# Two sums of x made one chunk later, and one `gl` made on GpSimd, in a fused attention and FFN kernel

## The chip, the cores and the metric

The kernel runs on one core of one Trainium2 chip. The metric is the device time of one execution in microseconds (us). Engines are named as the profile does: PE is TensorE (PEld its weight loads), DVE is VectorE, ACT is ScalarE, POOL is GpSimd, SP is SyncE, whose queue issues most DMAs.

## The reference

Linear attention over 8 batches, 8 heads, 576 positions and 64 columns, and a feed-forward layer over its 4608 rows of 512:

```python
q_s = exp(q - max(q, -1)); q_s = q_s / (sum(q_s, -1) + 1e-9)
k_s = exp(k - max(k, 2));  k_s = k_s / (sum(k_s, 2) + 1e-9)
x = q_s @ (k_s.T @ v)            # per batch and head; then 4608 x 512
h = maximum(x @ w_in, 0)         # 512 -> 2048
out = (h * h) @ w_out            # 2048 -> 512
```

All of it is float32.

## The kernel before, in words

**Split products.** A float32 value goes through TensorE as two parts, `hi` (rounded to the format fp32r, by a ScalarE copy) and `lo` (the rest, by a VectorE subtraction). A product of two values is three matmuls: hi x hi, hi x lo and lo x hi. So each operand of a matmul needs one ScalarE instruction and one subtraction before TensorE may read it.

**Tiles and chunks.** The rows are cut into nine tiles of 512: tile t below 8 holds the first 512 positions of batch t, and the ninth gathers the last 64 positions of all batches (`x_tail`). Tiles 0 to 6 go through the loop `for t in range(WT)` with sixteen chunks f of 128 hidden columns each. A chunk is `first` (the product with `w_in` into the PSUM tile `h`, twelve matmuls; then `r` = relu on ScalarE and `h` = relu(h) times r on VectorE), and two chunks later `second` (four times three matmuls into the four PSUM tiles `acc`), with `split_g` making `gh` on ScalarE and `gl` on VectorE as weights of `second`. Into these chunks the attention of the next batch is woven: `turns[t, f]` says which steps (b, s) are done in chunk f. In tile 6 the last of them, step 15 of batch 7, falls in chunk 11. There `step_between` multiplies x for the third pair of heads and splits q of the fourth (`blocks_split`: `qh` on ScalarE, `ql` on VectorE), and `step_after` multiplies x for the fourth pair. `x_product` makes six matmuls, copies one half of the result on ScalarE and the other on VectorE, and then copies 64 columns into `xt` on ScalarE.

**The joint block.** The last two tiles, 7 and 8, are not multiplied one by one. With both halves of the 512 columns of x, and the weights in quarters, seven products do the work of eight (a Strassen scheme). It needs sums of x: t1 = b12 - b11, t2 = b22 - t1, t3 = b11 - t2, t4 = b21 - t2, where b11 and b21 are halves of tile 7 and b12 and b22 halves of tile 8, and each is split into hi and lo. `ahead(f, x)` makes them in the last tile's chunks 4 to 15, at the end of each chunk's instructions; `take` is two VectorE subtractions of 128 x 512, and `split_x_of` two ScalarE casts and two VectorE subtractions. The temporary tiles of t1 are `sum_k` and `sum_q`; the profile calls the pieces of x after their split `w`, since they lie in memory of used weights.

The joint block itself is `for n in range(PAIRS)`, eight pairs of chunks. In a pair, seven `product` calls of six matmuls each (L1193) go into two PSUM tiles, and between them `unit` calls do the `second` products of the pair before, or, in the first pair, those of tile 6 that are left. `use_g` makes relu squared in place on VectorE (tile `c`), then `gh` on ScalarE and `gl` on the engine that it is given, for the two chunks that are used at once; `keep_g` writes the other two to memory for tile 8. The `gh` and `gl` of pair 0 are read first by the units of pair 1.

**What sets the order.** Tile 0 is ordered by a planner that simulates the engines (`Planner`). From tile 1 on each engine runs its instructions in the order in which the program states them, so a waiting instruction holds back all that stands behind it on its engine. Most instructions carry line 100 in the profile, the helper that issues them (the joint block's and the loop's), and are told apart by tile names.

Of the kernel before, what the change touches and what calls it, by code (L numbers as in the profile page):

```python
# [336 lines left out]
def attention_ffn(  # L337
# [75 lines left out]
    V, S, G = Engine(plan, nc.vector, 0.14, 0.00108), Engine(plan, nc.scalar, 0.18, 0.00087), Engine(plan, nc.gpsimd, 0.1, 0.0021)  # L413
# [693 lines left out]
    def weights(n):  # L1107

        if n >= PAIRS:
            return None  # L1110
        if n % 2 == 0:
            quads = [slabs[i].rearrange("p t (i c) -> p (t i) c", c=HM) for i in (0, 1, 14, 15)]
            w = {}
            for q, names in enumerate((("s1", "a11"), ("s2", "a12"), ("s3", "a22"), ("s4",))):
                for i, name in enumerate(names):
                    w[name] = quads[q][:, 2 * i:2 * i + 2, :]
        else:
            big = att.tile([P, 4, M], F32R, tag="x_next", name=f"ring_{n}")
            big = big.rearrange("p t (i c) -> p (t i) c", c=HM)
            w = {name: big[:, 2 * i:2 * i + 2, :] for i, name in enumerate(("s1", "a11", "s2", "a12"))}  # L1120
            for name, tag in (("s3", "qn"), ("a22", "qh"), ("s4", "ql")):
                w[name] = att.tile(
                    [P, 2, HM], F32R, tag=tag, name=f"ring_{name}_{n}", bufs=None if tag == "qn" else 1
                )
        return w
# [4 lines left out]
    def load_weights(n, w, *names):  # L1130

        for name in names if w else ():
            if n >= OWN and name in SUMS:
                continue
            at = SOURCE[name]
            Y.dma_start(out=w[name].bitcast(F32), in_=w_sums[n][:, at:at + 2, :])
# [52 lines left out]
    def product(out, w, x, begin, end=True):  # L1189
        (wh, wl), (xh, xl) = (w[:, 0, :], w[:, 1, :]), x  # L1190
        for k in range(2):
            for i, (a, m) in enumerate(((wh, xh), (wh, xl), (wl, xh))):
                nc.tensor.matmul(  # L1193
                    out=out.real(), lhsT=a[:, k * P:(k + 1) * P].real(), rhs=m[k].real(),
                    start=(begin and k == 0 and i == 0), stop=(k == 1 and i == 2),
                    skip_group_check=True,
                )
# [240 lines left out]
    def take(name, eng, out, in0, in1):  # L1438

        for i in range(2):  # L1440
            eng.tensor_tensor(out=out[i], in0=in0[i], in1=in1[i], op=ALU.subtract)
        made[name] = out

    def split_x_of(name):

        x_of[name] = pieces(name, 0)
        for i in range(2):
            split_part(made[name], name, i)

    def ahead(f, x):  # L1450

        k = range(2)
        if f == 4:
            made["b11"] = [x[:, i, :] for i in k]
            made["b21"] = [x[:, 2 + i, :] for i in k]
            made["b12"], made["b22"] = (
                [slabs[X_RAW + j].bitcast(F32)[:, i, :] for i in k] for j in range(2)
            )
            for i in k:
                to = slabs[X_RAW + i].bitcast(F32)[:, :, 0:(B - 1) * TL]  # L1460
                Y.dma_start(out=to, in_=x_tail[:, 2 * i:2 * i + 2, 0:(B - 1) * TL])
            w_of[0] = weights(0)
            load_weights(0, w_of[0], "a11", "s1", "a12", "s2")
        elif f == 6:
            split_x_of("b11")
        elif f == 10:
            temps = [att.tile([P, M], F32, tag=tag, name=f"sum_{tag}") for tag in ("k", "q")]
            take("t1", V, temps, made["b12"], made["b11"])
        elif f == 11:
            split_x_of("t1")  # L1470
        elif f == 12:
            split_x_of("b21")
            take("t2", V, made["t1"], made["b22"], made["t1"])
        elif f == 13:
            split_x_of("t2")
            take("t3", V, made["b11"], made["t2"], made["b11"])
        elif f == 14:
            split_x_of("t3")
            take("t4", V, made["b21"], made["b21"], made["t2"])
        elif f == 15:  # L1480
            load_weights(0, w_of[0], "s3", "a22", "s4")
            split_x_of("b22")
# [16 lines left out]
    for t in range(WT):  # L1499
        x_next, acc = begin_next(t), begin_acc(t)  # L1500
        parts = {}
        for f in range(NF):
# [29 lines left out]
            if t == WT - 1:  # L1532
                ahead(f, x_next)
# [12 lines left out]
    def unit(count):  # L1546

        for t, f, parts_u, acc_u, c, begin, end in units[:count]:
            second(f, parts_u, acc_u, c, begin=begin, end=end)
            if f == end:  # L1550
                store(t, acc_u, c)
        del units[:count]
# [6 lines left out]
    def use_g(f, c, tags, eng):  # L1559

        V.scalar_tensor_tensor(out=c, in0=c, scalar=0.0, in1=c, op0=ALU.max, op1=ALU.mult)
        split_last(f, c, tags, eng, WT)

    def split_last(f, c, tags, eng, t):

        gh, gl = (
            pool_of.tile([P, M], F32R, tag=tag, name=f"{kind}_{t}_{f}", bufs=bufs)
            for kind, (pool_of, tag, bufs) in zip(("gh", "gl"), tags)
        )
        S.copy(out=gh, in_=c)  # L1570
        eng.tensor_tensor(out=gl, in0=c, in1=gh, op=ALU.subtract)
        parts[t, f] = gh, gl

    one_tags = ((ffn, "gh", None), (ffn, "gl", None))
# [9 lines left out]
    for n in range(PAIRS):  # L1584
        one, two = 2 * n, 2 * n + 1
        units_at = (0, 1, 1, 1, 1) if n else (3, 0, 1, 0, 0)
        w = w_of.pop(n)
        w_next = w_of.get(n + 1)
        own_sums(n + 1, w_next, 0)
        A, Bk = (ps_h.tile([P, M], F32, tag="h", name=f"h_{WT}_{f}") for f in (two, one))  # L1590
        u1, u2, u3 = (
            ffn.tile([P, M], F32, tag=tag, name=f"u_{tag}_{n}", bufs=1) for tag in ("xh2", "xl2", "xh3")
        )
        c11, c21 = (ffn.tile([P, M], F32, tag="r", name=f"c_{WT}_{f}") for f in (one, two))
        c22, c12 = (att.tile([P, M], F32, tag="ek", name=f"c_{B}_{f}", bufs=2) for f in (two, one))
        if n == 0:
            split_x_of("t4")
        unit(units_at[0])

        product(A, w["a11"], x_of["b11"], True)  # L1600
        S.copy(out=u1, in_=A)
        unit(units_at[1])
        product(Bk, w["a12"], x_of["b21"], True)
        V.tensor_tensor(out=c11, in0=Bk, in1=u1, op=ALU.add)
        use_g(one, c11, one_tags, V)
        own_sums(n + 1, w_next, 1)
        if n == PAIRS - 1:
            load_g(0)
            load_g(1)
        unit(units_at[2])  # L1610
        product(A, w["s2"], x_of["t2"], False)
        S.copy(out=u2, in_=A)
        own_sums(n + 1, w_next, 2)
        if n == 0:
            w_of[1] = weights(1)
            load_weights(1, w_of[1], "a11", "s1", "a12", "s2", "s3", "a22", "s4")
        elif n + 2 < PAIRS:
            w_of[n + 2] = weights(n + 2)
        unit(units_at[3])
        product(Bk, w["s1"], x_of["t1"], True)  # L1620
        if n == 0:
            w_of[2] = weights(2)
        load_weights(n + 2, w_of.get(n + 2), "a12", "s2", "a11", "s1")
        own_sums(n + 1, w_next, 3)
        unit(units_at[4])
        product(A, w["s3"], x_of["t3"], False)
        S.copy(out=u3, in_=A)
        V.tensor_tensor(out=c22, in0=Bk, in1=u3, op=ALU.add)
        keep_g(two, c22)
        own_sums(n + 1, w_next, 4)  # L1630
        if n == PAIRS - 1:
            load_g(2)
        unit(2)
        product(A, w["a22"], x_of["t4"], False)
        load_weights(n + 2, w_of.get(n + 2), "s3", "a22")
        S.copy(out=c21, in_=A)
        own_sums(n + 1, w_next, 5)
        unit(1)
        product(Bk, w["s4"], x_of["b22"], False)
        load_weights(n + 2, w_of.get(n + 2), "s4")  # L1640
        V.tensor_tensor(out=c12, in0=Bk, in1=u2, op=ALU.add)
        tags = ((att, "v", 2), (att, "k" if n % 2 else "q", None))
        use_g(two, c21, tags, V)
        keep_g(one, c12)
        own_sums(n + 1, w_next, 6)
        if n == PAIRS - 1:
            load_g(3)
        unit(1)
        if acc is None:
            acc = begin_acc(WT)  # L1650
        units += [(WT, f, parts[WT, f], acc, c, 0, NF - 1) for f in (one, two) for c in range(C)]
# [54 lines left out]
```

## Time and profile before

| | |
|---|---|
| three runs | 876.64, 876.74, 879.33 us |
| median | 876.74 us |
| the profiled execution | 876.96 us, span 875.2 us |
| TensorE busy | 853.2 us |
| VectorE busy | 582.5 us |
| ScalarE busy | 379.4 us |
| GpSimd busy | 124.4 us |
| mean granted TensorE clock | 0.999 |

The span runs from the first to the last recorded instruction; the execution's own time is 1.76 us more. A row of a timeline gives start, duration, engine, line, operation, output and inputs, and in brackets how long the engine was idle before and who ended that. A row of a view of waits gives who waited for whom, microseconds in total, how often, and the longest. In a row of the chain that ended last, start and duration count only the part of an instruction that lies on the chain.

### The profile page before, as it was taken

What the parts mean: (1) busy time and instruction counts of PE and PEld (TensorE: products, weight loads), DVE (VectorE), ACT (ScalarE), POOL (GpSimd) and SP (SyncE); (2) the same over time, 40 slices, a digit from 0 to 9 for tenths busy, and PEclk for the clock granted to TensorE, in tenths of its full rate; (3) what the DMA queues carried; (4) which work ended last, traced back from release to release, by engine and by line L of the source; (5) the groups of instructions that cost most, each with busy time, mean ns of one, the idle gap of its engine ahead of it and who ended that gap; (6) DMA issues with size and microseconds to landing.
All of it is one profiled execution on the core that took longest, in us unless ns stands there. A gap on an engine that the chain in (4) does not pass through costs nothing.

```text
span 875.2 us, 12474 instructions
## 1 busy us (share of the span) xinstructions
PE 853.2 (97%) x4408; PEld 703.6 (80%) x4408; DVE 582.5 (67%) x1174; ACT 379.4 (43%) x731; POOL 124.4 (14%) x153
## 2 busy tenths in 40 slices
PE   5889999999999999999999999999999999999997
PEld 4668878888888888888888888888887888888786
DVE  5898896656766667667766566676677656766421
ACT  3888864343534253434534353334343442323321
POOL 4788991000000000000000000000000000000000
PEclk9999999999999999999999999999999999999999
DMA  9991022212331344132340332122341163332432
GB/s 279 382 347 45 25 68 73 76 38 75 93 98 29 87 106 134 39 83 80 95 105 21 87 90 52 27 54 64 87 121 31 38 204 109 105 102 69 156 113 49
DMA packets 157071, 86.08 MB, mean 98 GB/s; under 512 B 112720, under 2 KB 141392, under 8 KB 157008
## 3 DMA queue, kind: packets, MB, share of 16 engines
q1 hardware_dynamic: 155296, 83.97, 33.6%
q10 hardware_dynamic: 1712, 1.31, 0.6%
q8 instruction: 35, 0.57, 0.3%
q14 instruction: 28, 0.23, 0.1%
HBM read 60.16 MB, written 24.51 MB: 97 GB/s over the span
## 4 chain that ended last, share of the span: by engine, by line
PE 89%; DVE 4%; DMA 3%; SPq 3%; ACT 1%; issue 0%; DVEq 0%; ACTq 0%
PE acc L100 43%; PE h L100 32%; PE h L1193 9%; SPq L100 3%; PE x L100 3%; PE kv L100 2%; DMA raw<-in_moe_w_out_dram 1%; DMA q<-in_q_dram 1%; DVE bst L100 1%; DVE km L100 1%; DVE h L100 1%; DMA kt<-in_k_dram 0%; DVE gl L100 0%; DMA bst<-bst 0%; DVE q L100 0%
## 5 line engine op out<-in xcount | busy, mean ns | idle before, releaser
L100 PE MATMUL acc<-w,gh 128*128 128x512 f32 x1152 | 355.8, 390 | 0.0
L100 PE MATMUL h<-xh,w 128*128 128x512 f32 x896 | 295.8, 392 | 2.3 <-DVE gl L100 2.3
L100 PEld LDWEIGHTS acc<-w,gh 128*128 128x128 f32 x1152 | 214.7, 188 | 43.9 <-ACT gh L100 0.4
L100 PE MATMUL acc<-w,gl 128*128 128x512 f32 x576 | 224.2, 389 | 0.0
L100 PEld LDWEIGHTS h<-xh,w 128*128 128x128 f32 x896 | 168.2, 188 | 38.4 <-DVE gl L100 2.4
L100 PE MATMUL h<-xl,w 128*128 128x512 f32 x448 | 174.5, 389 | 0.0
L100 PEld LDWEIGHTS acc<-w,gl 128*128 128x128 f32 x576 | 108.1, 188 | 23.1 <-DVE gl L100 0.4
L100 DVE TENSOR_TENSOR gl<-h,gh 128x512 fp32r<-128x512 f32 x112 | 77.1, 689 | 71.2 <-ACT gh L100 61.7
L100 ACT ACTIVATE gh<-r 128x512 fp32r<-128x512 f32 x112 | 70.7, 631 | 92.7 <-PE acc L100 90.3
L100 DVE SCALAR_TENSOR_TENSOR h<-h,r 128x512 f32<-128x512 f32 x112 | 77.2, 690 | 45.2 <-ACT r L100 44.6
L100 PEld LDWEIGHTS h<-xl,w 128*128 128x128 f32 x448 | 84.1, 188 | 16.3
L100 ACT ACTIVATE r<-h 128x512 f32<-128x512 f32 x112 | 66.4, 593 | 65.2 <-PE h L100 64.9
L100 POOL PARTITION_ALL_REDUCE kmx<-km x24 | 16.9, 703 | 509.2 <-DVE km L100 509.2
L100 ACT ACTIVATE q<-q 128x576 f32<-128x576 f32 (+1 forms) x32 | 21.6, 674 | 70.3 <-DVE q L100 62.3
L100 DVE TENSOR_REDUCE bst<-q 128x18 f32<-128x576 f32 x48 | 35.9, 748 | 13.9 <-ACT q L100 13.5
L100 POOL TENSOR_TENSOR w<-w,raw 128x512 int32<-128x512 int32 x32 | 42.1, 1325 | 6.5 <-DVE w L100 3.7
L100 POOL TENSOR_TENSOR w<-w,w 128x512 fp32r<-128x512 f32 x32 | 41.1, 1299 | 4.7 <-ACT w L100 4.5
L100 DVE TENSOR_TENSOR q<-q,bst 128x576 f32<-128x576 f32 x48 | 36.4, 758 | 1.7
L100 ACT ACTIVATE raw<-raw 128x1024 f32<-128x1024 f32 (+1 forms) x32 | 36.3, 1148 | 0.1
L1193 PE MATMUL h<-w,w 128*128 128x512 f32 x144 | 36.0, 389 | 0.0
L100 DVE TENSOR_TENSOR bst<-bst 128x18 f32<-128x18 f32 (+1 forms) x96 | 17.8, 186 | 23.6 <-DMA bst<-bst 14.8
L100 DVE TENSOR_TENSOR ql<-qT,qh 128x576 fp32r<-128x576 f32 (+1 forms) x32 | 23.6, 739 | 14.1 <-ACT qh L100 12.9
(163 smaller groups left out, 893.6 us busy)
## 6 DMA issues: line engine op xcount, KB each, us to landing
k<-in_k_dram SPq DMA_DIRECT2D x32, 256.0 KB, 2.9
raw<-in_moe_w_in_dram SPq DMA_DIRECT2D x16, 512.0 KB, 8.7
raw<-in_moe_w_out_dram SPq DMA_DIRECT2D x16, 512.0 KB, 9.4
out_dram<-o SPq DMA_DIRECT2D x32, 256.0 KB, 2.4
w_sums<-w SPq DMA_DIRECT2D x30, 256.0 KB, 3.1
v<-in_v_dram SPq DMA_DIRECT2D x56, 128.0 KB, 3.0
q<-in_q_dram SPq DMA_DIRECT2D x96, 72.0 KB, 2.3
w<-w_sums SPq DMA_DIRECT2D x16, 256.0 KB, 3.7
```

The lines of the kernel that those rows point to most:

```text
L100: getattr(self.eng, op)(*map(real, args), **{k: real(a) for k, a in kwargs.items()})
L1193: nc.tensor.matmul(out=out.real(), lhsT=a[:, k * P:(k + 1) * P].real(), rhs=m[k].real(), start=(begin and k == 0 and i == 0), stop=(k == 1 ...
```

## The change

Two edits in the last stretch of the kernel. The `take` of t1 moves from the end of chunk 10 of tile 6 to the end of chunk 11, directly in front of t1's split, which was in chunk 11 already. And in the joint block's pair 0 the subtraction that makes `gl` of the pair's first chunk (`use_g(one, ...)`) is issued on GpSimd; in pairs 1 to 7 it stays on VectorE.

```diff
         elif f == 6:
             split_x_of("b11")
-        elif f == 10:
+        elif f == 11:
             temps = [att.tile([P, M], F32, tag=tag, name=f"sum_{tag}") for tag in ("k", "q")]
             take("t1", V, temps, made["b12"], made["b11"])
-        elif f == 11:
             split_x_of("t1")
         elif f == 12:
             split_x_of("b21")
...
         V.tensor_tensor(out=c11, in0=Bk, in1=u1, op=ALU.add)
-        use_g(one, c11, one_tags, V)
+        use_g(one, c11, one_tags, V if n else G)
         own_sums(n + 1, w_next, 1)
```

## The prediction

> **What bounds the kernel now.** I read the page first, for the share of each engine; then TensorE's waits from the last batch's end on; then the chain that ended last around the place of the change; then the timelines of TensorE, VectorE and ScalarE there. The page:
>
> ```profile
> span 875.2 us, 12474 instructions
> ## 1 busy us (share of the span) xinstructions
> PE 853.2 (97%) x4408; PEld 703.6 (80%) x4408; DVE 582.5 (67%) x1174; ACT 379.4 (43%) x731; POOL 124.4 (14%) x153
> ```
>
> TensorE is busy for 97% of the span, VectorE for 67%, GpSimd for 14%. So VectorE's time counts only where TensorE waits for it. All waits of TensorE's matmuls from 660 us to the end of the span:
>
> ```profile
> PE x L100 <- ACT qh L100: 0.5, 1, 0.5
> PE x L100 <- DVE ql L100: 0.3, 1, 0.3
> ```
>
> There are two, both at the last product of x (tile `x`, of `x_product`) before the joint block. Everything else after 660 us runs back to back on TensorE; what makes these two shorter ends the kernel earlier, and nothing else there does. The chain that ended last says what they hang on (start, duration, what):
>
> ```profile
> 674.22 0.69 DVE sum_k L100
> 674.91 0.60 DVE sum_q L100
> 675.51 0.03 issue
> 675.54 0.70 DVE h L100
> 676.24 0.30 DVE x L100
> 676.57 0.21 ACT xt L100
> 676.80 0.68 ACT qh L100
> 677.51 0.77 DVE ql L100
> ```
>
> `sum_k` and `sum_q` are the "first two sums of x": the two subtractions of `take("t1")`. They stand on VectorE in front of chunk 11's `h` and of the copy of `x`. The copy releases `xt` on ScalarE, behind `xt` stands `qh`, behind `qh` comes `ql` on VectorE, and TensorE needs `qh` and `ql`. So the sums are on the path that sets the end, from 674.22 to 675.51: 1.29 us. TensorE meanwhile (start, duration):
>
> ```profile
> 674.68 0.29 PE L100 MATMUL x<-ql,kvh 128*128 128x288 f32 x1
> ...
> 676.65 0.39 PE L100 MATMUL acc<-w,gl 128*128 128x512 f32 x1
> 677.53 0.40 PE L100 MATMUL x<-qh,kvh 128*128 128x288 f32 x1 [0.49 <-ACT qh L100]
> ...
> 678.32 0.40 PE L100 MATMUL x<-ql,kvh 128*128 128x288 f32 x1 [0.26 <-DVE ql L100]
> ...
> 678.95 0.40 PE L100 MATMUL h<-xh,w 128*128 128x512 f32 x1
> ```
>
> From the start of the last `acc` matmul (676.65) to chunk 12's first `h` matmul (678.95) it takes 2.30 us. The same stretch, undisturbed by sums, stands in the trace at the product of the same batch's other two pairs of heads, some chunks earlier:
>
> ```profile
> 640.30 0.39 PE L100 MATMUL acc<-w,gl 128*128 128x512 f32 x1
> 640.53 0.29 PE L100 MATMUL x<-qh,kvh 128*128 128x288 f32 x1
> 640.66 0.29 PE L100 MATMUL x<-qh,kvl 128*128 128x288 f32 x1
> 640.83 0.40 PE L100 MATMUL x<-ql,kvh 128*128 128x288 f32 x1
> ...
> 641.47 0.39 PE L100 MATMUL h<-xh,w 128*128 128x512 f32 x1
> ```
>
> There the same six matmuls and the step to `h` take 641.47 - 640.30 = 1.17 us. Their `ql` was made here:
>
> ```profile
> 638.65 0.39 DVE L100 COPY x<-x 128x224 f32<-128x224 f32 x1
> 640.01 0.76 DVE L100 TENSOR_TENSOR ql<-qT,qh 128x576 fp32r<-128x576 f32 x1 [0.97 <-ACT qh L100]
> ```
>
> **The change part by part. First part, the sums one chunk later.** What is taken out of chunk 11 is 1.29 us of VectorE in front of `h`. How early can the chain then start? ScalarE's rows around it:
>
> ```profile
> 673.60 0.60 ACT L100 ACTIVATE r<-h 128x512 f32<-128x512 f32 x1
> ...
> 679.69 0.62 ACT L100 CAST w<-sum_k 128x512 fp32r<-128x512 f32 x1
> 680.21 0.62 ACT L100 CAST w<-sum_q 128x512 fp32r<-128x512 f32 x1
> 681.88 0.60 ACT L100 ACTIVATE r<-h 128x512 f32<-128x512 f32 x1 [1.05 <-PE h L100]
> 684.44 0.63 ACT L100 ACTIVATE gh<-r 128x512 fp32r<-128x512 f32 x1 [1.96 <-PE acc L100]
> ```
>
> Chunk 11's `r` ends at 674.20, and VectorE comes free for the first sum at 674.22; so `h` can start there instead, near 674.24, and end near 674.94. The copy of `x` after it needs the `x` matmul of 674.68, which ends at 674.97: the copy starts near 675.02, set by TensorE now and no longer by VectorE. In the undisturbed block, from the start of the copy (638.65) to the end of `ql` (640.77) it is 2.12 us, which holds the rest of the copy, `xt`, `qh` and `ql`. That puts the end of `ql` at 677.14. TensorE used it 0.06 us after its end there, so at 677.20 here. Measured from the last `acc` matmul: there 640.83 - 640.30 = 0.53 us; here 676.65 + 0.53 = 677.18. The two agree within 0.02 us, so I take the undisturbed block as the model for the whole stretch: chunk 12 starts at 676.65 + 1.17 = 677.82 in place of 678.95. The gain is 1.13 us.
>
> Both ends: at best `ql` does not bind at all, and the six matmuls follow at the step of 640.53 to 640.66, 0.13 us, after a first step of 0.23 (640.30 to 640.53); 0.23 + 6 x 0.13 = 1.01 us, a gain of 1.29. At the low end only the idle time that the view of waits names is won, 0.49 + 0.26 = 0.75 us; the rest, 0.38 us, is the slower start of the pipelined matmuls after each halt, which should go with the halts. Below nothing this term can't go unless the sums cost more at their new place, which comes next.
>
> The Trainium skill says the same about idle time of TensorE (Perfetto Trace Analysis, Identifying the Most-Contended Engine): busy time of matmuls is a poor measure, since pipelined instructions look smaller. By busy time alone the sum would be 0.75 us, by starts it is 1.13; the trace's own rows above show the difference.
>
> What the sums cost at the new place: they now stand in chunk 11's `ahead`, behind the last copy of `x` and in front of their own split; all of it is VectorE and ScalarE work, there are no DMAs with them, and no queue of SP or GpSimd is passed. Behind them on VectorE: the two `lo` subtractions, then chunk 12's `h`. Behind the casts on ScalarE: chunk 12's `r`. The copy's row of before is
>
> ```profile
> 679.16 0.39 DVE L100 COPY x<-x 128x224 f32<-128x224 f32 x1 [0.29 <-PE x L100]
> ```
>
> Moved by 1.13 it ends at 678.42. The sums then take 678.45 to 679.74 by the 1.29 above. The casts wait for them one by one: the first may start near 679.2, the second near 679.77, and it ends near 680.4. Chunk 12's `r` waited for TensorE until 681.88; moved, that is 680.75. So ScalarE is free 0.35 us before it is wanted, and the cost is nothing. If that cover were gone, the next one is the wait of 1.96 us in front of `gh` (684.44), where ScalarE waits for TensorE: the sums would have to come 2.3 us later than reckoned before anything that TensorE reads moved.
>
> **Second part, `gl` of chunk 0 of the joint block on GpSimd.** It takes one instruction from VectorE and gives it to GpSimd:
>
> ```profile
> 707.91 0.69 DVE L100 TENSOR_TENSOR gl<-c,gh 128x512 fp32r<-128x512 f32 x1 [0.74 <-ACT gh L100]
> 711.06 0.69 DVE L100 TENSOR_TENSOR c<-h,u_xh 128x512 f32<-128x512 f32 x1 [2.46 <-ACT u_xh L100]
> ```
>
> After this `gl` VectorE has nothing to do until 711.06, where it waits for ScalarE's `u_xh` and so for TensorE. Taking 0.69 us from it there gains nothing. GpSimd's price of the same shape, and the use of this `gl`:
>
> ```profile
> L100 POOL TENSOR_TENSOR w<-w,w 128x512 fp32r<-128x512 f32 x32 | 41.1, 1299 | 4.7 <-ACT w L100 4.5
> 717.27 0.19 PEld L100 LDWEIGHTS acc<-w,gl 128*128 128x128 f32 x1
> ```
>
> On GpSimd it takes 1.30 us, twice as long: 707.91 + 1.30 = 709.21, and TensorE loads it as a weight first at 717.27, in the next pair. That leaves 8.06 us, which moves with TensorE and so stays. Nothing else is queued on GpSimd there, and VectorE is idle while it runs. The cost is nothing; the cover is those 8.06 us.
>
> **The sum.** -1.13 for the sums, 0 for their new place, 0 for `gl`. The profiled execution took 876.96 us with a span of 875.2, so 1.76 lies around the span. Forecast for it: span 874.07, time 875.83. It stands 0.22 above the median of the runs, 876.74; less 1.13 this gives 875.6.
>
> **The rivals.** First: the halt goes only in part. The copy of `x` could start later than 675.02, since the matmuls in front of it hang on the `kv` parts made just before, and each 0.1 us there costs 0.1. For it speaks that `ql` would arrive within 0.02 us of the moment that it is needed, so there is no room; against it, that the undisturbed block has the same order of work and its `ql` matmul comes only 0.04 us later than the step of 0.13. A gain from 0 to 0.75: 876.0 to 876.7.
>
> Second: the gain is given back, because something that does not move with TensorE turns up late in the joint block, a load of weights say. For it: TensorE would be 1.13 us earlier at every load. Against it: TensorE has not one wait after 678.32 in the view of waits, and loads that refill buffers wait for their readers, which come earlier too. 876.7.
>
> Third, slower: GpSimd brings `gl` too late. This happens at the first second-product of the joint block's chunk 0, at 717.27; it decides from 8.06 us of delay on, each microsecond beyond costs one, and with the 1.13 won before, the kernel is slower than now only from 9.19 us on, and by over 0.3% from 11.8 us on. For it: GpSimd has had no such subtraction since the weights were split. Against it: by the row above, the thirty-two like it took 1299 ns on average, so the delay would have to be over six times the instruction.
>
> The Trainium skill has a rule for this (GPSIMD Engine Reference, Instruction dispatch): the first call to freshly loaded code pays about 6 us that no row shows. By that estimate `gl` would still come 2 us early and the sum is the same; no run here shows such a load for a subtraction after a long pause.
>
> **How the numbers follow.** Forecast 0.83, first rival 0.10, second 0.05, third 0.02. What a measurement of this kernel can tell from no change is about 0.3%, 2.6 us; no case but the third reaches it. So: within 0.3% 0.95; slower 0.03, the third rival and a little for scatter, since one of the three runs of before stands at 879.33; faster 0.02, for something that no row shows. Range: at the low end the best gain from the lowest run, 876.64 - 1.29 = 875.35, and 0.15 for scatter, 875.2; at the high end no gain, 876.74, rounded up to 876.8, which takes in the first two rivals.
>
> **What would show it.** Right: the two waits of `x` on `qh` and `ql` gone or under 0.1 us together, some 1.2 us from the last `acc` matmul to chunk 12's `h`, `sum_k` behind the last copy of `x`, all of TensorE's later work 1.1 us earlier, and one `gl` of about 1.3 us on GpSimd that ends over 7 us before its weight load. Wrong: a wait for `ql` of 0.3 us or more (first rival); a new wait of TensorE in the joint block (second); `acc` waiting for GpSimd's `gl` (third); chunk 12's `r` or `h` late behind the casts, which would break the step on the new place.

## The result and the profile after

The changed kernel takes 872.14 us, median of six runs (870.65 to 874.13); before it was 876.75 (876.49 to 879.33). The ratio is 0.9944, interval 0.9925 to 0.9963. Forecast were 875.6 us, range 875.2 to 876.8, no measurable difference: 4.6 us were won where 1.1 were reckoned, and the time lies below the range. The profiled execution took 870.65 us with a span of 868.9, against 876.96 and 875.2. So 6.3 us of span have to be found. They are more than the 4.6 us of the medians because the profiled execution is the fastest of its six, 1.5 us under their median; the two longest, 873.63 and 874.13 us, had a granted clock of 0.995, the others 0.997 to 1.0.

First the place that the prediction spoke of. The timeline of TensorE after, the rows that answer to those of before:

```profile
671.57 0.39 PE L100 MATMUL acc<-w,gl 128*128 128x512 f32 x1
671.79 0.29 PE L100 MATMUL x<-qh,kvh 128*128 128x288 f32 x1
671.92 0.29 PE L100 MATMUL x<-qh,kvl 128*128 128x288 f32 x1
672.11 0.40 PE L100 MATMUL x<-ql,kvh 128*128 128x288 f32 x1
...
672.75 0.40 PE L100 MATMUL h<-xh,w 128*128 128x512 f32 x1
```

From the last `acc` matmul to chunk 12's `h` it is 1.18 us; before it was 2.30, forecast was 1.17. Both waits are gone, and TensorE has none left from 640 us to the end. VectorE there:

```profile
669.14 0.70 DVE L100 SCALAR_TENSOR_TENSOR h<-h,r 128x512 f32<-128x512 f32 x1
669.93 0.39 DVE L100 COPY x<-x 128x224 f32<-128x224 f32 x1
671.30 0.76 DVE L100 TENSOR_TENSOR ql<-qT,qh 128x576 fp32r<-128x576 f32 x1 [0.98 <-ACT qh L100]
672.49 0.69 DVE L100 TENSOR_TENSOR gl<-h,gh 128x512 fp32r<-128x512 f32 x1 [0.43 <-ACT gh L100]
673.10 0.38 DVE L100 COPY x<-x 128x224 f32<-128x224 f32 x1
673.39 0.68 DVE L100 TENSOR_TENSOR sum_k<-w,x 128x512 f32<-128x512 f32 x1
674.00 0.68 DVE L100 TENSOR_TENSOR sum_q<-w,x 128x512 f32<-128x512 f32 x1
```

`sum_k` and `sum_q` stand behind the last copy of x, as they should. This explains 1.12 of the 6.3 us. The rest was there before any changed line ran. The last all-reduce on GpSimd lies ahead of both edits; it starts at 660.66 before and 655.55 after, 5.11 us apart. The very first one, before and after, is 5.16 apart:

```profile
143.15 0.72 POOL L100 PARTITION_ALL_REDUCE kmx<-km  x1 [7.86 <-DVE km L100]
```

```profile
137.99 0.73 POOL L100 PARTITION_ALL_REDUCE kmx<-km  x1 [7.86 <-DVE km L100]
```

So the difference comes from the opening. Rows from GpSimd's start, before, and after:

```profile
0.72 0.20 POOL masks.py:197 MEMSET ident<- 128x128 f32 x1 [0.29 <-POOLq L1686]
9.45 0.28 POOL masks.py:199 TENSOR_SCALAR_AFFINE_SELECT ident<-ident 128x128 f32<-128x128 f32 x1 [8.53 <-issue]
```

```profile
0.72 0.20 POOL masks.py:197 MEMSET ident<- 128x128 f32 x1 [0.29 <-POOLq L1685]
1.22 0.29 POOL masks.py:199 TENSOR_SCALAR_AFFINE_SELECT ident<-ident 128x128 f32<-128x128 f32 x1 [0.29 <-POOL ident masks.py:197]
```

Before, GpSimd stood still for 8.53 us in front of the affine select that makes the identity, and the profile names nothing that it waited for ("issue"). After, the pause is 0.29 us. TensorE needs the identity for all that it does first, so this pause was its longest wait in the whole kernel. The view of TensorE's waits over the whole span, before and after:

```profile
PE idle L1383 <- POOL ident masks.py:199: 9.8, 1, 9.8
PE h L100 <- DVE gl L100: 2.3, 2, 2.0
```

```profile
PE h L100 <- DVE gl L100: 2.4, 2, 2.0
PE kT L100 <- DMA k<-in_k_dram: 2.1, 2, 1.2
PE idle L1383 <- POOL ident masks.py:199: 1.6, 1, 1.6
PE qT L100 <- POOL ks L100: 0.9, 1, 0.9
```

The 9.8 us become 1.6, 8.2 less. Not all of it comes through: the transposes of k now wait for k to land (2.1 us in two waits), which the pause had hidden. TensorE's second group of transposes of k starts 4.66 us earlier (8.89 against 13.55), the first `h` matmul 5.24 us earlier (27.44 against 32.68), and 5.16 is what is left at the first all-reduce.

And `gl` on GpSimd:

```profile
701.77 1.29 POOL L100 TENSOR_TENSOR gl<-c,gh 128x512 fp32r<-128x512 f32 x1 [45.51 <-ACT gh L100]
```

It takes 1.29 us as reckoned, and TensorE loads it 8.0 us after its end:

```profile
711.07 0.19 PEld L100 LDWEIGHTS acc<-w,gl 128*128 128x128 f32 x1
```

Why should a change near the end shorten the start? The order of GpSimd's instructions in the two compiled programs gives a hint. In front of the affine select, of the first all-reduce and, after the change, of `gl`, there stands one more instruction without operands, put in by the compiler. The last work of GpSimd in after:

```
PartitionAllReduce        kmx_7_3_6482 <- km_7_3_6479
PseudoReloadLibraryIndex  index 0
TensorTensor              gl_7_0_6867 <- c_7_0_6862, gh_7_0_6865
```

The first entry is the last all-reduce, the second the added instruction under the compiler's own name; before, the work ends with the all-reduce. In both programs it stands in front of the affine select with index 0, and in front of the first all-reduce with index 1.

**Theory.** The all-reduce on one side and the affine select and the subtraction on the other need different code on GpSimd, and the instruction without operands changes it, if the other code is there. What is there at the end of one execution is there at the start of the next. Before, each execution ended on the all-reduce's code and the next had to change it in front of the affine select, with TensorE waiting. After, `gl` makes the change late in the kernel, while GpSimd has 45 us of nothing to do. **Rivals:** `gl`'s place on VectorE was worth the time after all; any late instruction on GpSimd does it; the number of instructions or changes does it, or chance; the sums did it.

### The profile page after: what moved, and what is told of

The parts are those of the page before. It is cut to its first block, busy times and chain, and to the rows that moved or that the text cites. A ratio compares the mean times of both kernels' runs of the same rounds, so it can differ in the third digit from the quotient of the medians.

```text
span 868.9 us, 12477 instructions
## 1 busy us (share of the span) xinstructions
PE 853.2 (98%) x4408; PEld 704.4 (81%) x4408; DVE 582.1 (67%) x1173; ACT 379.9 (44%) x731; POOL 126.0 (14%) x154
## 4 chain that ended last, share of the span: by engine, by line
PE 92%; DVE 4%; DMA 1%; ACT 1%; issue 1%; SPq 1%; POOL 0%; DVEq 0%; ACTq 0%; POOLq 0%
PE acc L100 44%; PE h L100 33%; PE h L1193 9%; PE x L100 3%; PE kv L100 2%; DMA raw<-in_moe_w_in_dram 1%; SPq L100 1%; DVE gl L100 0%; DVE qt L100 0%; DVE h L100 0%; DMA kt<-in_k_dram 0%; DVE w L100 0%; DVE km L100 0%; DVE up L100 0%; DVE bst L100 0%
```

## The experiments

Each kernel was timed beside the kernel before on the same chip. In all of them two numbers of the trace are read: the pause in front of the affine select, and the step from the last `acc` matmul to chunk 12's `h`.

**The sums alone.** Against after:

```diff
-        use_g(one, c11, one_tags, V if n else G)
+        use_g(one, c11, one_tags, V)
```

> Only the two sums are moved; gl stays on VectorE. Theory (code on GpSimd): an execution that ends with the all-reduce's code on GpSimd pays a pause of about 8.5 us in front of the first affine select of the next one, and this kernel still ends that way: pause 8.5 us, x to h step of about 1.2 us, time 1.1 us under before, 875.6. Rival (the sums change more than was reckoned): pause gone, time near 872.

Measured: 875.80 us, ratio 0.9984 (0.9975 to 0.9994). The step is 1.19 us, the pause is there:

```profile
8.67 0.28 POOL masks.py:199 TENSOR_SCALAR_AFFINE_SELECT ident<-ident 128x128 f32<-128x128 f32 x1 [7.75 <-issue]
```

So the first half of the change does what the prediction said and no more: 1.4 us by the medians, 0.5 to 2.2 by the interval.

**`gl` alone.** Against before:

```diff
-        use_g(one, c11, one_tags, V)
+        use_g(one, c11, one_tags, V if n else G)
```

> Only gl of pair 0 goes to GpSimd; the sums stay. Theory (code on GpSimd): the subtraction brings its code back before the execution ends, so the pause of 8.5 us in front of the affine select is gone; some 5.1 us of it reach the end: 871.6, with the two waits for qh and ql still there. Rival (VectorE's relief, or chance): 876.7 and the pause as before.

Measured: 873.29 us, ratio 0.9953 (0.9938 to 0.9968), 3.9 us less than before. The pause is 0.29 us, and the two waits of 0.5 and 0.3 us for `qh` and `ql` are still there. It is 1.7 us slower than forecast; the opening is where that lies, below. This half of the change, reckoned at nothing, is the larger one.

**A one-column instruction in place of `gl`, twice.** `gl` stays on VectorE, and GpSimd does something at the same place of its order that no one needs (into `pad`, a tile that no one reads, which this and the later edits only give a name): a copy, in front of which the compiler puts nothing, or an addition, in front of which it puts the instruction without operands. Both against before:

```diff
         use_g(one, c11, one_tags, V)
+        if n == 0:
+            G.tensor_copy(out=pad[:, 0:1], in_=zeros[:, 0:1])
```

> As before, with a one-column copy on GpSimd at the place where gl would be; in front of it the compiled program has no instruction that changes GpSimd's code. Theory (code on GpSimd): pause of 8.5 us stays, 876.7. Rival (any late instruction on GpSimd does it): pause gone, 871.6.

```diff
         use_g(one, c11, one_tags, V)
+        if n == 0:
+            G.tensor_tensor(out=pad[:, 0:1], in0=zeros[:, 0:1], in1=zeros[:, 0:1], op=ALU.add)
```

> As before, with a one-column addition on GpSimd at the place where gl would be; in front of it the compiled program has the instruction that changes GpSimd's code. gl stays on VectorE. Theory (code on GpSimd): pause gone, 871.6. Rival (VectorE's relief): pause of 8.5 us, 876.7.

Measured: with the copy 877.37 us, ratio 0.9999 (0.9989 to 1.0008); with the addition 872.81 us, ratio 0.9952 (0.9936 to 0.9967). The affine select with the copy, and with the addition:

```profile
8.95 0.28 POOL masks.py:199 TENSOR_SCALAR_AFFINE_SELECT ident<-ident 128x128 f32<-128x128 f32 x1 [8.03 <-issue]
```

```profile
1.21 0.29 POOL masks.py:199 TENSOR_SCALAR_AFFINE_SELECT ident<-ident 128x128 f32<-128x128 f32 x1 [0.29 <-POOL ident masks.py:197]
```

VectorE's relief falls, since here it has none, and so does "any late instruction". The timelines also show what the theory takes for the change of code, at a place where the DMA queues are nearly idle; the copy behind the last all-reduce, then the addition behind it:

```profile
660.65 0.70 POOL L100 PARTITION_ALL_REDUCE kmx<-km  x1 [16.30 <-DVE km L100]
661.23 0.25 POOL L100 COPY pad<-zeros 128x1 f32<-128x1 f32 x1
```

```profile
655.26 0.70 POOL L100 PARTITION_ALL_REDUCE kmx<-km  x1 [16.27 <-DVE km L100]
663.08 0.18 POOL L100 TENSOR_TENSOR pad<-zeros 128x1 f32<-128x1 f32 x1 [7.12 <-issue]
```

The copy follows at once; the addition, which waits for nothing either, comes 7.12 us later, again "issue". The same pause as at the start, at a place where it costs nothing.

**The all-reduce's code brought back.** Against after:

```diff
         use_g(one, c11, one_tags, V if n else G)
+        if n == 0:
+            G.partition_all_reduce(pad[:, 0:1], zeros[:, 0:1], channels=P, reduce_op=RED.max)
```

> As after, with one more all-reduce of one column on GpSimd behind gl, which nothing waits for. Theory (code on GpSimd): the execution ends with the all-reduce's code again, the pause of about 8.5 us is back, and the time is that of the moved sums alone: 875.6. Rival (gl's place on VectorE was the cost): 871, no pause.

Measured: 875.89 us, ratio 0.9987 (0.9979 to 0.9996). `gl` runs on GpSimd as in after, 1.28 us, the step at x is 1.20 us, and the pause is back. The all-reduce behind `gl` has a pause of its own, 7.33 us. The affine select and that all-reduce:

```profile
8.90 0.28 POOL masks.py:199 TENSOR_SCALAR_AFFINE_SELECT ident<-ident 128x128 f32<-128x128 f32 x1 [7.98 <-issue]
715.48 0.38 POOL L100 PARTITION_ALL_REDUCE pad<-zeros  x1 [7.33 <-issue]
```

All of the change is in this kernel, and its ratio lies where that of the sums alone does, at 0.9984.

**The addition in the middle.** Against before:

```diff
         G.partition_all_reduce(kmx, km, channels=P, reduce_op=RED.max)
+        if b == 4 and p == 0:
+            G.tensor_tensor(out=pad[:, 0:1], in0=zeros[:, 0:1], in1=zeros[:, 0:1], op=ALU.add)
```

> As before, with the one-column addition on GpSimd in the middle, behind the first all-reduce of batch 4: two changes of GpSimd's code more, but the execution still ends with the all-reduce's. Theory (what is there at the end decides): pause of 8.5 us, 876.7; the two changes hide in the 20 us between all-reduces. Rival (the number of changes or instructions decides): pause gone, 871.6.

Measured: 877.08 us, ratio 1.0004 (0.9995 to 1.0013), pause 7.76 us. GpSimd at the start and in the middle:

```profile
8.68 0.28 POOL masks.py:199 TENSOR_SCALAR_AFFINE_SELECT ident<-ident 128x128 f32<-128x128 f32 x1 [7.76 <-issue]
330.76 0.70 POOL L100 PARTITION_ALL_REDUCE kmx<-km  x1 [27.95 <-DVE km L100]
338.32 0.18 POOL L100 TENSOR_TENSOR pad<-zeros 128x1 f32<-128x1 f32 x1 [6.86 <-issue]
348.98 0.73 POOL L100 PARTITION_ALL_REDUCE kmx<-km  x1 [10.47 <-DVE km L100]
```

One change of 6.86 us is seen; the change back can lie unseen in the 10.47 us before the next all-reduce, and TensorE has no wait between 150 and 640 us, as before. Two changes more cost and help nothing that is measured. What stands last decides.

**The change of code put on the path.** Against after:

```diff
     def use_g(f, c, tags, eng):
...
         V.scalar_tensor_tensor(out=c, in0=c, scalar=0.0, in1=c, op0=ALU.max, op1=ALU.mult)
+        if eng is G:
+            G.partition_all_reduce(pad[:, 0:1], c[:, 0:1], channels=P, reduce_op=RED.max)
```

> As after, with an all-reduce of one column of c directly in front of gl on GpSimd, so that the change of code cannot be done ahead and stands between c and gl. It measures the price of the change: theory (the pause at the start is this change): gl starts about 8 us after the all-reduce, and TensorE, which has some 8 us, waits for it between 0 and 1 us; time 871 to 872.5. Rival (the pause at the start is something else): gl starts within 1 us, time as after.

Measured: 874.47 us, ratio 0.9969 (0.9957 to 0.9981), slower than forecast. GpSimd, and TensorE's wait:

```profile
702.39 0.39 POOL L100 PARTITION_ALL_REDUCE pad<-c  x1 [44.78 <-DVE c L100]
712.90 1.25 POOL L100 TENSOR_TENSOR gl<-c,gh 128x512 fp32r<-128x512 f32 x1 [10.13 <-ACT o L100]
```

```profile
714.21 0.50 PE L100 MATMUL acc<-w,gl 128*128 128x512 f32 x1 [1.43 <-POOL gl L100]
```

`gl` starts 10.1 us after the all-reduce's end (its `gh` was ready at 703.0, so the `o` that the row names is only what ended last), and TensorE waits 1.43 us for it. This is the prediction's third rival, made to happen: the cover of some 8 us is real, and this pause was longer than it. The forecast had 0 to 1 us for that wait; besides, the first all-reduce stands at 139.34 us here, 1.35 later than in after, which belongs to the scatter of the opening. The pause at the start is 0.29 us, since the execution ends on the subtraction's code.

**Sums and addition.** Like `tt_last`, with the sums moved.

> The sums moved, gl on VectorE, and the one-column addition on GpSimd. Theory (code on GpSimd): the same as after, 870.6 to 872, since gl's own place is worth nothing. Rival (gl's place is worth something): slower than after by what it is worth.

Measured: 871.51 us, ratio 0.9937 (0.9925 to 0.9950). The interval holds after's ratio, 0.9944. `gl`'s own place is worth nothing that can be measured: a one-column addition does all that it did.

## Why the prediction was wrong

**The sums: right.** `h`, the copy, `qh` and `ql` moved up, the undisturbed block was the right model (1.18 us against 1.17), the waits are gone, and the new place cost nothing: chunk 12's `r` came on TensorE's `h`, as forecast. The term was 1.13 us, the trace has 1.12, the kernel with the sums alone 1.4 by its medians. What the Trainium skill says of TensorE (Perfetto Trace Analysis, Identifying the Most-Contended Engine) is that the busy time of its matmuls is a poor measure of how near it is to its peak, as pipelined ones look smaller in the trace. This trace fits that: the waits that went sum to 0.75 us, and the step became 1.12 us shorter.

**`gl` on GpSimd: the step that failed.** The prediction's words were "Nothing else is queued on GpSimd there, and VectorE is idle while it runs. The cost is nothing". The instruction's own cost is nothing indeed (1.29 us, 8.0 us of cover), but the term of the sum is not: this half alone gives 3.9 us, and a one-column addition in its place 4.4. What failed is that only the moved instruction was priced, and not what the compiler puts in front of it, nor what it leaves behind for the next execution. The row that would have said it was in the profile of before: TensorE's longest wait, 9.8 us for `ident`, behind an "issue" of GpSimd. The prediction looked at the waits from 660 us on, found two, and wrote that nothing else could end the kernel earlier "there"; the opening was never read. Its chance of 0.02 for faster was for "something that no row shows"; this row showed it.

**The price of a load.** The rule of the Trainium skill (GPSIMD Engine Reference, Instruction dispatch: about 6 us at the first call to freshly loaded code, with no row) was cited as a danger to `gl` alone. If the pause is such a load, it was already being paid at the start of the profiled execution of before. The trace agrees with it in kind; the pauses measured are longer, 6.9 to 7.2 us where the DMA queues were nearly idle.

**Rivals.** The first and second did not come: no wait of TensorE is left after 640 us. The third came only where it was built. None was a gain elsewhere, so the range had no room for one.

**The sum, put right:** 1.12 at x and 5.16 in the opening are 6.28 of the 6.3 us between the two profiled spans. By the medians it is 4.6; where the other executions of after lost the rest, no profile shows.

**What is shown and what is not.** Shown is that the pause at the start follows the kind of GpSimd's last instruction: an all-reduce last gives 7.75 to 8.53 us (before, the sums alone, `copy_last`, where the copy has no change in front of it, `tt_mid`, `reduce_last`), a subtraction or addition last gives 0.29 us (after, `gl_only`, `tt_last`, `reduce_before_gl`, `sums_tt`). In all ten compiled programs the added instruction stands in front of the affine select with index 0, so the openings are alike; the last index in the program is 1 in the five with the pause and 0 in the five without. That it is code that stays loaded from one execution to the next is the reading that fits these ten profiles and the compiler's name for its instruction. It is not shown directly. No view shows the loading; in the 7.2 us of `tt_last`'s pause 0.03 MB moved in all. And no record says which kernel ran ahead of a profiled execution.

Open is why the gain differs between executions. Without the pause the first all-reduce starts at 137.8 to 139.8 us in the five profiles, with it at 142.5 to 143.4. `gl_only` is the latest, 1.82 us behind after, and yet the two are level (55.53 us) at TensorE's transpose of `km`. Then VectorE waits 0.85 us for a load of q at 68.89, its row `km<-km,kt` takes 1.40 us against 0.28, its `gl` comes late, and TensorE has two waits that after lacks, 0.30 us at 73.45 and 0.81 at 74.89. So part of the difference arises behind the pause, in tile 0; why that load and that row took longer was not tried.

## What to carry to other kernels

Read the waits of the critical engine over the whole span before the place of an edit: the longest one is worth a line of the sum even when the edit is at the other end. An instruction given to another engine can bring along what the compiler puts in front of it, and can leave a state behind, so look at that engine's whole order, its last instruction and its first ones, and at every "issue" pause. If GpSimd does two kinds of work, let it end on the kind that it starts with, and make the change where it has nothing to do: here one column of an addition does it.

## What the runs showed of the hardware

GpSimd's pause between an all-reduce and a two-input addition took 6.86, 7.12 and 7.17 us where little DMA ran (`tt_mid`, 37 GB/s; `tt_last`, 4; `sums_tt`, 6). Between the all-reduce and the subtraction in the joint block it took 10.1 us (303 GB/s), from the subtraction to the all-reduce there 7.33 us (321 GB/s), so traffic alone doesn't order these numbers. In front of the affine select at the start it took 7.75 to 8.53 us (247 GB/s in before). The pause is not tied to its instruction's waits: in after, `gl` started at 701.77 as its `gh` came, 45.5 us behind the all-reduce, and no pause followed that wait. A copy ran straight behind the all-reduce (`copy_last`, 661.23), and before the memset at 0.72 us ran ahead of the pause.
